# Pairs of tokens in VectorE's transposes, and a way by DRAM for decayed k in twelve units instead of six

## Chip, core and metric

The kernel runs on one core of a Trainium2 chip. Its time is the device time of one execution in microseconds. Five engines work on their own instruction streams and meet through semaphores: PE (TensorE, matmuls and transposes into PSUM), DVE (VectorE), ACT (ScalarE), POOL (GpSimd) and SP (SyncE, which here only issues DMAs).

## What is computed

Two parts follow each other. The first is a gated linear attention over 4 sequences of 768 tokens with 8 heads of width 48:

```
f = sigmoid(f_logit)
state = f[t] * state + k[t] v[t]^T          # one 48 x 48 state per head, token by token
y[t] = q[t] @ state
```

The second is a feed-forward block on the result, laid out as 3072 tokens of width 384, with a hidden width of 1536:

```
g = x @ w_gate
out = (silu(g) * (x @ w_val)) @ w_out
```

Both parts are computed in fp32 and the output is fp32.

## The kernel before

**Chunks and units.** The sequence is cut into 6 chunks of 128 tokens (numbered 0 to 5), and a unit is one batch element of one chunk: unit u = 4 x chunk + batch, 24 in all. `attention(u)` is a generator: each `yield` ends a step, and the caller decides where in the stream of the feed-forward work the next step is put. The recurrence over a chunk becomes matmuls: with cumulative products of the gates, k is scaled by the product of the gates that follow it ("decayed k", tile `kT`) and q by the running product (`qT`), and then scores = kT x qT, masked by `causal`, give `A`; y comes from A x v and from qT x the decayed state.

**From tokens to columns.** The arrays come with tokens on the partitions; the scans and the matmuls want head dimensions on the partitions and tokens along the row. In chunks 0 and 1 PE does those transposes. From chunk 2 on (`SQUARES = 2`) DVE does: it transposes squares of 32 x 32, so the DMA loads f, k and q into `rooms` ("fsquares", "ksquares", "qsquares"), one room each, in such a way that a token t lies at partition and square (t, i) with token number 4t + i. `in_turn` is the view of the output that puts the tokens back into their order: the next element of a transposed row is written four fp32 further on.

**The steps of a unit from chunk 2 on**, each with its line:
- L556 (ACT) sigmoid of the f squares; L565 (DVE) transposes them into `gates`
- L572 (DVE) transposes the k squares into `kT`
- L576 (DVE) the scan from the end of the chunk, into `tails`; L579 a reciprocal
- L584 (DVE) kT = kT x tails
- if the unit is `turned`: L591 (DVE) transposes the squares of kT into `beside`, which is the memory of this unit's qT, and L594 (SP) writes that to the DRAM tile `turn` in four DMAs, in runs of 32 fp32. Units 14 to 19 are turned
- L598 (DVE) the scan from the front, into `gates`
- L601 (DVE) transposes the q squares into `qT`; then `load_after(u)` puts the twelve DMAs for the f, k and q squares of the next unit on SP (L428)
- L604 (DVE) qT = qT x gates, and a small memset on POOL (L605)
- L617 (PE) the scores; in a unit that is not turned, L621 (PE) also transposes kT back to tokens on partitions
- the decayed k with tokens on the partitions, `kt`, comes from PSUM by ACT (L629), or, in a turned unit, from `turn` by one DMA (L627)
- L631 (DVE) the mask; L540 (DVE) the decayed state
- y (L652, L656 on PE for batches 0 to 2, copied by ACT at L660 into `yT` and moved into xT by ten DMAs on SP at L667; L677 on PE for batch 3, which uses `diagonal`, a tile that shares its memory with yT and that POOL clears at L544 and ACT fills at L546)
- L697 (PE) dS = kt x v, the addition to the state; the v of the unit after next is loaded (L432)

`kT` and `kt` have one buffer each, `qT` two, and the rooms one each.

**The feed-forward.** From chunk 1 on, gate and val are computed by fifteen block products in place of eighteen (`mlp_fifteen`, PE at L957): the sums of tokens (`xs`), the sums of weights (`extra`) and the combination of the products (`c`, `aside`, then `h` at L909) are made by DVE (L858, L861, L864) and ACT (L962, L973). The second matrix works by seven products in place of eight (`down_seven`, PE at L1056 and L1119). This is called a block below: block c computes the feed-forward of chunk c, and the attention of chunk c + 1 is put into it.

**What sets the order.** Tables of planned times (`CHAINS`, `SCORES`) give the place of each attention step within the block. All instructions that are traced from there on are then held in that order on PE, DVE, ACT, POOL and SP (`keep_order`). [...]

```
    in_order(mark, (mybir.EngineType.PE, mybir.EngineType.DVE, mybir.EngineType.Activation,
                    mybir.EngineType.Pool, mybir.EngineType.SP))
```

Of the kernel before, what the change touches and what calls it, by code (L numbers as in the profile page):

```python
# [13 lines left out]
ALU = mybir.AluOpType  # L14
# [275 lines left out]
def short_path(ctx, tc, ident, least, judge, q, k, v, f_logit, moe_w_gate, moe_w_val, moe_w_out, out):  # L290
# [9 lines left out]
    nc = tc.nc  # L300
    B, H, S, D = q.shape
    C = 128
    NCH = S // C
    HP = H // 2
# [6 lines left out]
    N1 = C + 1  # L311
# [3 lines left out]
    SQUARES = 2  # L315
# [47 lines left out]
    def pairs(t, off=0):  # L363
        return t[:, off:off + HP * N1].rearrange("p (a t) -> p a t", t=N1)
# [30 lines left out]
    NI = C // Q  # L395
    RUN = NI * D

    rooms = {}
# [9 lines left out]
    def squares(nm):  # L408
        return rooms[nm][:, Q:Q + HP * RUN].rearrange("t (a i e) -> t a i e", a=HP, i=NI)[:, :, :, 0:Q]

    def in_turn(t):

        return t.rearrange("p a (t i) -> p a i t", i=NI)

    def load(u, what="fkqv"):
        b, c = units[u]
        rows = slice(c * C, (c + 1) * C)
        for nm, src in (("f", f_logit), ("k", k), ("q", q), ("v", v)):
            if nm not in what:
                continue  # L420
            if nm == "v":
                dst = v_of(u)
            elif c < SQUARES:
                dst = raw[nm][u % NRAW]
            else:
                for n in range(4):
                    at = Q * (1 - n % 2)
                    nc.sync.dma_start(  # L428
                        out=rooms[nm][Q * n:Q * (n + 1), at:at + HP * RUN].rearrange("t (a e) -> t a e", a=HP),
                        in_=src[b, n // 2::2, rows, :].rearrange("a (t i) d -> t a (i d)", i=NI))  # L430
                continue
            nc.sync.dma_start(out=dst[:, :, 0:D], in_=src[b, :, rows, :].rearrange("h t d -> t h d"))  # L432
# [79 lines left out]
    def rows_of(par):  # L512
        return slice(W * par, W * par + D)
# [3 lines left out]
    def bank(name):  # L517
        return banks[-1].tile([128, 512], FP32, tag="a", name=name)
# [10 lines left out]
    def attention(u):  # L529
        b, c = units[u]  # L530
        fr, kr, qr = (raw[nm][u % NRAW] for nm in "fkq")
        v_ = v_of(u)
        gate, tail = (x[u % NROT if c < SQUARES else 0] for x in (gates, tails))

        diagonal = None

        def decay():
            nonlocal diagonal
            if c:
                nc.vector.tensor_tensor(decayed[:, :, 0:D], states[b], whole.broadcast_to((128, HP, D)), ALU.mult)  # L540
            if c and b == B - 1:

                diagonal = att.tile([128, HP, 2 * D], FP32, tag="x", name="diagonal")
                nc.gpsimd.memset(diagonal, 0.0)  # L544
                for par in range(2):
                    nc.scalar.copy(diagonal[rows_of(par), :, par * D:(par + 1) * D], decayed[rows_of(par), :, 0:D])  # L546

        def transposed(name, src):
            p = bank(name)
            for a in range(HP):  # L550
                nc.tensor.transpose(p[:, a * C:(a + 1) * C],
                                    src[:, 2 * a:2 * a + 2, :].rearrange("t r d -> t (r d)"), ident)
            return p.rearrange("p (a t) -> p a t", t=C)
# [6 lines left out]
        else:  # L560
            p = transposed("fTp", fr)
            nc.scalar.activation(pairs(gate)[:, :, 1:N1], p, AF.Copy if u in ahead else AF.Sigmoid)
        yield
        if c >= SQUARES:
            nc.vector.transpose(in_turn(pairs(gate)[:, :, 1:N1]), squares("f"))  # L565
        yield

        kT = att.tile([128, HP, C], FP32, tag="kT", name="kT")
        qT = att.tile([128, HP, C], FP32, tag="qT", name="qT", bufs=2)
        kp, qp = kT, qT  # L570
        if c >= SQUARES:
            nc.vector.transpose(in_turn(kT), squares("k"))  # L572
        yield

        n = HP * N1
# [5 lines left out]
        if c < SQUARES:  # L581
            kp = transposed("kTp", kr)
            qp = transposed("qTp", qr)
        nc.vector.tensor_tensor(kT, kp, pairs(tail, 2)[:, :, 0:C], ALU.mult)  # L584
        yield
        turned = (SQUARES + 1) * B + 1 < u < (NCH - 1) * B
        if turned:


# [8 lines left out]
        nc.vector.tensor_tensor_scan(gate[:, 0:n], gate[:, 0:n], start, 1.0, op0=ALU.mult, op1=ALU.add)  # L598
        yield
        if c >= SQUARES:  # L600
            nc.vector.transpose(in_turn(qT), squares("q"))  # L601
            load_after(u)
        yield
        nc.vector.tensor_tensor(qT, qp, pairs(gate)[:, :, 1:N1], ALU.mult)  # L604
        nc.gpsimd.memset(pairs(gate)[:, :, 0:1], 0.0)  # L605
        if 0 < c < SQUARES:
            load_after(u)
        if c < SQUARES:
            decay()
# [8 lines left out]
        if c < NCH - 1 and not turned:  # L618
            p = bank("kt")
# [14 lines left out]
        if c >= SQUARES:  # L634
            decay()
# [4 lines left out]
        if c and b < B - 1:  # L640
# [20 lines left out]
            for h in range(H):  # L661
                a, par = h // 2, h % 2
# [31 lines left out]
        if c < NCH - 1:  # L694
            p = bank("dS")
# [13 lines left out]
    def load_after(u):  # L709

        w = u + (1 if units[u][1] >= SQUARES else 2)
        if w < len(units) and (units[w][1] >= SQUARES) == (w == u + 1):
            load(w, "fkqv" if units[w][1] < SQUARES or w == SQUARES * B else "fkq")

    def attention_steps(c):

        runs = [attention(c * B + b) for b in range(B)]
        parts = [3, 6, 3, 3]
        order = sorted((2 * b + s, b, n) for b in range(B) for s, n in enumerate(parts))
        return [lambda b=b, n=n: [next(runs[b]) for _ in range(n)] for _, b, n in order]  # L720
# [445 lines left out]
    mark = traced[-1]  # L1166
    keep_warm(5)
    first = [attention(b) for b in range(B)]
    done = [0] * B

# [82 lines left out]
    for c in range(2, NCH):  # L1253
        for b in range(B):
            run = attention(c * B + b)
            waiting += [((c - 2) * whole + t, lambda run=run: next(run)) for t in times(c)[b]]
# [33 lines left out]
def kernel(  # L1290
# [22 lines left out]
    def judge(bank):  # L1313
# [12 lines left out]
        yield  # L1326

    short_path(tc, ident, least, judge, *args)
    with tc.If(redo[0] > 0):
        general_path(tc, *args)  # L1330
# [32 lines left out]
```

## Time and profile before

| | us |
|---|---|
| median of 3 runs | 610.28 |
| lowest and highest | 609.24, 611.36 |
| the profiled execution, its time | 611.44 |
| the profiled execution, its span | 609.6 |
| PE busy in the span | 595.8 |
| DVE busy | 494.3 |
| ACT busy | 288.5 |
| POOL busy | 7.6 |

The granted clock of PE was 0.996. Times of single instructions come from the profiled execution, counted from the start of its span. Instructions on one engine overlap by about 0.1 us in the records, so the distance between two starts is what an instruction takes of its engine: a 128 x 512 addition on DVE lasts 0.69 us and the next starts 0.60 us after it.

A line of the groups reads: line, engine, operation, output<-input, shapes, count | busy us, mean ns of one | idle time of the engine just before, and what ended it. A line of a timeline reads: start, duration, engine, line, operation, output<-input, count, and in brackets the idle time before it and what ended it. A line of the chain reads: start, us, engine and line. SPq is SP's queue of DMA issues.

### The profile page before, as it was taken

How to read it: one execution, taken by the hardware profiler on the slowest of the kernel's cores; microseconds unless marked ns; L12 is line 12 of the kernel's file. 1: busy time of each engine (PE TensorE's matmuls, PEld its weight loads, DVE VectorE, ACT ScalarE, POOL GpSimd, SP SyncE). 2: the span in 40 equal slices, each digit the busy share in tenths (PEclk: the TensorE clock that was granted, in tenths of full speed). 3: DMA queues.
4: the chain of work that ended last, by engine and by line, in shares of the span. 5: the costliest groups of instructions: out<-in, count | busy, mean ns of one | idle time of the engine just before them, and what ended most of it. 6: DMA issues, size and time to landing. Idle time of an engine off the chain costs nothing.

```text
span 609.6 us, 10796 instructions
## 1 busy us (share of the span) xinstructions
PE 595.8 (98%) x4036; PEld 491.1 (81%) x4036; DVE 494.3 (81%) x833; ACT 288.5 (47%) x554; POOL 7.6 (1%) x52
## 2 busy tenths in 40 slices
PE   7899999999999999999999999999999999999996
PEld 5744545667888799888899988899988899988896
DVE  7999989868999985999996789996878981566731
ACT  3466644313776522476732366742276730366600
POOL 1000000000000000000000000000000000000000
PEclk9999999999999999999999999999999999999999
DMA  9988372005312044323236334145313100100001
GB/s 199 260 194 295 126 247 79 5 15 159 95 39 70 23 108 115 105 53 96 61 89 145 94 97 110 35 112 120 110 44 90 27 6 10 53 1 1 0 1 59
DMA packets 109142, 54.10 MB, mean 89 GB/s; under 512 B 68760, under 2 KB 102168, under 8 KB 109080
## 3 DMA queue, kind: packets, MB, share of 16 engines
q1 hardware_dynamic: 107064, 50.56, 31.3%
q10 hardware_dynamic: 2016, 2.75, 1.2%
q8 instruction: 34, 0.56, 0.4%
q14 instruction: 28, 0.23, 0.1%
HBM read 44.04 MB, written 6.29 MB: 83 GB/s over the span
## 4 chain that ended last, share of the span: by engine, by line
PE 85%; DVE 10%; SPq 1%; issue 1%; DMA 1%; ACT 1%; POOL 0%; DVEq 0%; ACTq 0%; POOLq 0%
PE o L1056 17%; PE A L957 15%; PE B L957 12%; PE gate L755 5%; PE val L755 5%; PE o L957 5%; PE c L957 5%; PE sc L617 4%; PE o L778 3%; PE o L1119 3%; PE y L677 2%; PE y L656 2%; PE dS L697 2%; PE y L652 1%; DVE c L861 1%
## 5 line engine op out<-in xcount | busy, mean ns | idle before, releaser
L1056 PE MATMUL o<-w_out,h 128*128 128x192 f32 x360 | 62.0, 327 | 0.5 <-DVE h L909 0.5
L957 PE MATMUL A<-xs,w_both 128*128 128x256 f32 x240 | 62.1, 381 | 0.0
L1056 PEld LDWEIGHTS o<-w_out,h 128*128 128x128 f32 x360 | 58.7, 190 | 1.7 <-DVE h L909 0.8
L962 ACT COPY c<-A 128x512 f32<-128x512 f32 x40 | 23.3, 583 | 62.6 <-PE A L957 62.6
L962 ACT COPY aside<-A 128x512 f32<-128x512 f32 x60 | 35.1, 584 | 32.6 <-PE A L957 32.6
L858 DVE TENSOR_TENSOR c<-c,aside 128x512 f32<-128x512 f32 x60 | 41.6, 694 | 10.5 <-ACT aside L962 9.0
L957 PEld LDWEIGHTS A<-xs,w_both 128*128 128x128 f32 x240 | 44.9, 190 | 6.5
L909 DVE TENSOR_TENSOR h<-h,c 128x256 f32<-128x256 f32 x100 | 41.1, 419 | 7.3 <-ACT h L973 7.3
L861 DVE TENSOR_TENSOR c<-c,aside 128x512 f32<-128x512 f32 x60 | 41.4, 689 | 2.5 <-ACT aside L962 2.5
L973 ACT ACTIVATE h<-c 128x256 f32<-128x256 f32 x100 | 39.2, 416 | 8.4 <-DVE c L858 5.8
L1056 PE MATMUL o<-ws,h 128*128 128x192 f32 x240 | 41.5, 328 | 0.2 <-DVE A L631 0.2
L957 PE MATMUL B<-xs,w_both 128*128 128x256 f32 x160 | 41.2, 380 | 0.6 <-ACT aside L962 0.6
L957 PE MATMUL c<-xT,w_both 128*128 128x256 f32 x160 | 41.2, 380 | 0.5 <-DVE c L861 0.5
L957 PE MATMUL A<-xs,extra 128*128 128x256 f32 x160 | 41.2, 380 | 0.0
L957 PE MATMUL B<-xT,extra 128*128 128x256 f32 x160 | 41.1, 379 | 0.0
L962 ACT COPY aside<-B 128x512 f32<-128x512 f32 x60 | 35.1, 584 | 11.7 <-PE B L957 7.2
L631 DVE TENSOR_TENSOR A<-sc,causal 128x512 f32<-128x512 f32 x48 | 30.8, 684 | 11.3 <-PE sc L617 11.3
L1056 PEld LDWEIGHTS o<-ws,h 128*128 128x128 f32 x240 | 39.1, 190 | 0.8 <-DVE A L631 0.4
L861 DVE TENSOR_TENSOR c<-o,c 128x512 f32<-128x512 f32 x40 | 27.6, 690 | 10.0 <-ACT h L973 5.8
L957 PEld LDWEIGHTS c<-xT,w_both 128*128 128x128 f32 x160 | 30.3, 190 | 5.0 <-DVE c L861 0.9
L957 PEld LDWEIGHTS B<-xs,w_both 128*128 128x128 f32 x160 | 30.2, 190 | 5.0 <-ACT aside L962 1.0
L957 PEld LDWEIGHTS A<-xs,extra 128*128 128x128 f32 x160 | 30.3, 190 | 4.5 <-ACT c L962 0.4
(138 smaller groups left out, 1140.2 us busy)
## 6 DMA issues: line engine op xcount, KB each, us to landing
fsquares<-in_f_logit_dram SPq DMA_DIRECT2D x64, 96.0 KB, 2.6
ksquares<-in_k_dram SPq DMA_DIRECT2D x64, 96.0 KB, 2.3
qsquares<-in_q_dram SPq DMA_DIRECT2D x64, 96.0 KB, 2.2
v<-in_v_dram SPq DMA_DIRECT2D x24, 192.0 KB, 3.0
w<-in_moe_w_gate_dram SPq DMA_DIRECT2D x6, 768.0 KB, 6.3
w<-in_moe_w_val_dram SPq DMA_DIRECT2D x6, 768.0 KB, 5.1
w<-in_moe_w_out_dram SPq DMA_DIRECT2D x6, 768.0 KB, 5.3
out_dram<-ob ACTq DMA_DIRECT2D x14, 192.0 KB, 2.7
```

The lines of the kernel that those rows point to most:

```text
L617: nc.tensor.matmul(sc[par][:, a * C:(a + 1) * C], lhsT=kT[r, a, :], rhs=qT[r, a, :], start=True, stop=True)
L631: nc.vector.tensor_tensor(A[:, par], sc[par].rearrange("p (a t) -> p a t", t=C), causal.unsqueeze(1).broadcast_to((128, HP, C)), ALU.mult)
L755: nc.tensor.matmul(p, lhsT=w[:, j, i, :], rhs=xT[c][:, i, :], start=(i == 0), stop=(i == KT - 1))
L778: nc.tensor.matmul(p, lhsT=hidden_tile(h, n // 2)[:, n % 2 * 2 + b // 2, b % 2 * C:(b % 2 + 1) * C], rhs=w_out[:, j, :], start=(n == 0), s ...
L858: nc.vector.tensor_tensor(dst, a, b, ALU.add)
L861: nc.vector.tensor_tensor(dst, a, b, ALU.subtract)
L909: lagging.append(lambda: f(*args))
L957: nc.tensor.matmul(p[name][:, n, :], lhsT=weights_of[a][:, n, j, :], rhs=tokens[b], start=fresh and n == 0, stop=True, skip_group_check=True)
L962: nc.scalar.copy(t, p[name])
L973: nc.scalar.activation(dst, src[:, 0, :], AF.Silu)
L1056: nc.tensor.matmul(p[:, n, :], lhsT=lhsTs[j][:, n * C:(n + 1) * C], rhs=rhs[:, j, :], start=first and j == order[0] and n == 0, stop=j == ...
L1119: nc.tensor.matmul(p, lhsT=hidden_tile(h, j)[:, 2, n * C:(n + 1) * C], rhs=b22[:, j, :], start=j == order[0], stop=j == order[-1])
```

## The change

- `split_squares` and `parted` replace the old views in the transposes of k and q: the output of a transpose is laid out as two halves j, each with (head pair, t, i) and i running over 2. Tokens lie in pairs, and the next element of a transposed row is written two fp32 further on. f is transposed as before.
- k is transposed into qT's memory instead of kT's; q into the memory of the k room instead of qT's.
- The products (`multiply`) read the paired layout, take their three operands in the order (head pair, t, j, i), and write kT and qT in the order of the tokens.
- `turned` holds for units 8 to 19.
- `load_after(u)`, with the loads of the next unit's squares, stands after q's product instead of after q's transpose.

```diff
+    def split_squares(nm):
+        return squares(nm).rearrange("t a (j i) e -> t a j i e", j=2)
...
+    def parted(t):
+        return t.rearrange("p (j a t i) -> p a j i t", j=2, a=HP, i=NI // 2)
...
+        def multiply(out, x, by):
+            if c >= SQUARES:
+                for_each = "p a (t j i) -> p a t j i"
+                out, by = (t.rearrange(for_each, j=2, i=NI // 2) for t in (out, by))
+                x = x.rearrange("p (j a t i) -> p a t j i", j=2, a=HP, i=NI // 2)
+            nc.vector.tensor_tensor(out, x, by, ALU.mult)
...
         if c >= SQUARES:
-            nc.vector.transpose(in_turn(kT), squares("k"))
+            kp = qT.rearrange("p a t -> p (a t)")
+            nc.vector.transpose(parted(kp), split_squares("k"))
...
-        nc.vector.tensor_tensor(kT, kp, pairs(tail, 2)[:, :, 0:C], ALU.mult)
-        yield
-        turned = (SQUARES + 1) * B + 1 < u < (NCH - 1) * B
+        multiply(kT, kp, pairs(tail, 2)[:, :, 0:C])
+        yield
+        turned = SQUARES <= c < NCH - 1
...
         if c >= SQUARES:
-            nc.vector.transpose(in_turn(qT), squares("q"))
-            load_after(u)
-        yield
-        nc.vector.tensor_tensor(qT, qp, pairs(gate)[:, :, 1:N1], ALU.mult)
+            qp = rooms["k"][:, 0:HP * C]
+            nc.vector.transpose(parted(qp), split_squares("q"))
+        yield
+        multiply(qT, qp, pairs(gate)[:, :, 1:N1])
         nc.gpsimd.memset(pairs(gate)[:, :, 0:1], 0.0)
-        if 0 < c < SQUARES:
+        if c:
             load_after(u)
```

On the engines' streams this takes 24 transposes off PE and 6 copies off ACT, adds 6 transposes on DVE, and adds 30 DMAs on SP (24 `turn<-qT`, 6 `kt<-turn`). On SP each unit's turn DMAs stand before the loads of the next unit's squares, and its kt DMA after them (after the xT and v DMAs too, where those follow). In unit 12 the load of v for unit 13 now stands before the squares of unit 13.

## The prediction

> **What bounds the kernel now.** I read the page first, busy shares and the chain that ended last; then the groups of instructions by form, the chain in order of time, and timelines of single engines around the units (unit = 4 x chunk + batch; chunks 2 to 4 are units 8 to 19). Busy shares, then the chain's shares by engine:
>
> ```profile
> PE 595.8 (98%) x4036; PEld 491.1 (81%) x4036; DVE 494.3 (81%) x833; ACT 288.5 (47%) x554; POOL 7.6 (1%) x52
> PE 85%; DVE 10%; SPq 1%; issue 1%; DMA 1%; ACT 1%; POOL 0%; DVEq 0%; ACTq 0%; POOLq 0%
> ```
>
> PE is full almost throughout; its order is written out, so it has nothing to put in place of an instruction that waits. Whatever takes PE work away gains, and whatever comes late for PE costs its whole delay. The groups:
>
> ```profile
> L572 DVE STREAM_TRANSPOSE kT<-ksquares 128x512 f32<-128x512 f32 x16 | 17.8, 1113 | 0.0
> L601 DVE STREAM_TRANSPOSE qT<-qsquares 128x512 f32<-128x512 f32 x16 | 18.0, 1125 | 6.4 <-DMA turn<-qT 6.4
> L591 DVE STREAM_TRANSPOSE qT<-kT 128x512 f32<-128x512 f32 x6 | 4.2, 702 | 0.0
> L629 ACT COPY kt<-kt 128x512 f32<-128x512 f32 x14 | 8.2, 585 | 16.7 <-PE kt L621 16.7
> ```
>
> L591 writes 32-element rows and takes 702 ns; L572 and L601 write every fourth element and take 0.41 us more. L601 also waited 6.4 us for `turn` to be written: that is the price of the way by DRAM. DVE's timeline shows these waits, SP's the queue ahead of them (unit 14, then 16):
>
> ```profile
> 275.14 2.63 SPq L594 DMA_DIRECT2D turn<-qT  x4
> 279.52 1.15 DVE L601 STREAM_TRANSPOSE qT<-qsquares 128x512 f32<-128x512 f32 x1 [0.58 <-DMA turn<-qT]
> ...
> 321.75 2.61 SPq L594 DMA_DIRECT2D turn<-qT  x4
> 328.31 1.13 DVE L601 STREAM_TRANSPOSE qT<-qsquares 128x512 f32<-128x512 f32 x1 [2.69 <-DMA turn<-qT]
> ```
>
> From the first issue of `turn` until DVE may write qT again, call it T: 4.4 us for unit 14, 6.6 for 16 (SP full before it), 6.2 for 17, at most 4.7 for 18. Last, the end of chunk 2 in the chain of waits, where SP itself is the path:
>
> ```profile
> 223.99 1.09 PE sc L617 x16
> 228.05 1.43 SPq L667
> 233.34 1.79 DMA xT<-yT
> 236.17 2.12 PE y L677 x56
> ```
>
> SP issues without a pause from 213.1 to 235: ten xT pieces of unit 9, v, twelve squares, ten xT pieces of unit 10 (226.85, 7.08 us). When these have landed POOL clears `diagonal` (235.31), ACT fills it, and PE's y of unit 11 starts at 236.17, having waited 0.3.
>
> [...] L473, reading every second word, takes 554 ns for 384 columns and 956 for 768, 1.05 ns a column. Writes at step two are not in the trace. [...] `turn` goes in 128 B runs and lands 3.1 us after an issue, q squares (768 B) after 2.2.
>
> **The change, part by part.**
>
> *32 transposes of k and q.* Bounds 0.70 (L591) and 1.11 us; I take 0.70. Start to start that is 0.95 to 0.60: 0.35 less each, 11 us of DVE. It hardly reaches PE, whose stalls lie in 178 to 210 (30.46 of 32 us busy) and about nowhere later. The 32 products read pairs: 0.69 as before[...].
>
> *kt of units 8 to 13 leaves PE and ACT.* In the chain, unit 8 with PE's transposes, then unit 18 without:
>
> ```profile
> 158.30 1.09 PE sc L617 x16
> 159.98 1.73 PE A L957 x8
> ...
> 385.67 1.09 PE sc L617 x16
> 386.76 1.06 PE A L957 x4
> 387.82 0.86 PE B L957 x4
> ```
>
> With them 0.59 lies between scores and next product; without, that product takes 0.20 more. Saved: 0.39 a unit, 2.35 for six. ACT's six copies (3.5 us) I count as nothing: ACT is 47% busy and PE there waits for none of them. POOL keeps its instructions.
>
> *What comes in:* six L591 transposes (0.60 a start on DVE), 24 turn and 6 kt DMAs on SP (2.63 + 0.67 us a unit), and three new orders. q's product, no longer q's transpose, waits for `turn`; behind it stand DVE's additions, the mask and, on PE, the scores. k and q loads of the next unit wait for q's product, because its room holds q; behind them on SP stand xT, v, kt and the next turn. k's transpose writes qT, free once y of two units earlier is done: everywhere so, counted as nothing.
>
> *Unit 8.* k's product starts 0.35 earlier (151.46), two additions, then L591 from 153.4 to 154.1. SP is idle, so T = 5.0 (between 4.4 and 6.2): q's product at 159.15, not 157.39. Its scores started 0.84 after it (158.23); now 160.0. **+1.75** (+1.15 to +3.35).
>
> *Units 8 and 9 without kt:* **-0.78**. In 178 to 209 DVE sets the pace; unit 10 there has two transposes less 0.35 and one more of 0.60, -0.1 net; DVE starts that stretch with its mask +1.36, so PE's second 0.39 is mostly lost: **+0.3**. The shift at 209 is 1.26; below, times are those of before, with the shift left out.
>
> *Unit 11.* SP first finishes unit 9's xT and v (220.9), then kt of unit 10, and reaches turn at 221.7. SP was full, as before unit 16: T = 6.6, q's product at 228.3, scores at 229.1 in place of 223.92. It doesn't end there. Unit 12's k loads wait for that product: 229.05, k and q 3.75, xT of unit 10 from 232.8 instead of 226.85. `diagonal`, and with it y of unit 11, comes 5.95 later: **+5.9**. PE's own delay and kt of units 10 and 11 (0.78) disappear under it. Of the 5.9, 3.3 are the five DMAs put in front of xT. With T = 4.4 and xT issued at 0.59 a piece it is +2.5. kt of unit 11 is issued at about 240.5, in time for 244.
>
> *Unit 12:* turn from 241, q's product near 246.6. State, outputs and token sums are behind it; those have 1.7 us of slack to PE: 0. *Unit 13:* k's product at 254.5, turn at 256.45, T = 5.0, scores at 262.3 instead of 261.7: +0.6, which swallows unit 12's 0.39; unit 13's comes off: **+0.2**. *Unit 16:* k loads wait for 312.2 instead of issuing at 306.1, so xT and turn go 2.3 later; scores 331.45 instead of 331.22: **+0.3**. Units 14 to 19 lose waits of 6.4 us on DVE that PE did not feel: 0.
>
> Sum: 1.75 - 0.78 + 0.3 + 5.9 + 0.2 + 0.3 = **+7.65 us**. The profiled execution took 611.44 (span 609.6), hence 619.1; the median of the runs is 1.16 lower, so I forecast 617.9.
>
> **The rivals.**
> - *Main case, slower by 4.5 to 9 us* (614.8 to 619.3): 0.55.
> - *Shallow:* T = 4.4 everywhere, SP as quick as elsewhere: 1.15 - 0.78 + 0.3 + 2.5 - 0.8 = +2.4, 612.7. For it: units 14 and 18. Against: unit 16, with the same queue ahead of it. From +1.8 to +4.5: 0.20.
> - *Deep:* T = 6.6 everywhere (+1.6 at unit 8, +1.6 at unit 13), and transposes that stay at 1.11 us (the change not doing what it says: +0.35 at units 8 and 13 and +0.7 at unit 10, where DVE paces): +12, 622. 0.12.
> - *Faster:* DVE gets to q's product after `turn` has landed and SP has room. Then PE's 2.35 comes in, with up to 1.5 of DVE stalls: 606.4 to 607.9. It decides at T under 3.3 us in unit 8 (154.15 to 157.4), and a turn for unit 11 issued by 218. Against it: three earlier issues take 2.0 us and the shortest landing seen is 2.1. 0.08.
> - *No change,* gains and waits cancelling within 0.3% (1.8 us, about what a measurement of this kernel can tell from no change): 0.05.
>
> Range 612.0 to 621.8: from the shallow end to nearly the deep one; left out are the faster and unchanged cases and the last of the deep one, 0.19.
>
> **What would show it.** Right: transposes of k and q near 0.70; no kt matmuls after unit 7; q's products of units 8 and 11 waiting for `turn`, 2 and 5 us or more; scores of unit 11 and then its y waiting on PE, DMA xT and SPq in the chain between them; PE busy less by 2 to 6 us. Wrong: y of unit 11 without a wait of some us, or a PE gap anywhere after chunk 3 that is larger than 2 us.

## The result, and the profile after

| | us |
|---|---|
| changed kernel, median of 7 runs | 624.88 (624.16 to 629.87) |
| kernel before beside it, median of 7 runs | 610.37 (609.24 to 611.36) |
| ratio, with its 95% interval | 1.0255 (1.0235 to 1.0274) |
| the profiled execution of the changed kernel, its span | 629.87, 628.1 |

The changed kernel is slower by 2.55%, about 15.6 us at 610.4 (14.5 by the medians); the forecast was 7.65. The profiled execution is the longest of the seven. Its granted clock was 0.982, that of the others 0.987 to 0.992, so its sums are some 5 us larger than the median's.

Busy shares, the granted clock in 40 slices and the chain by engine, from the page of the changed kernel:

```profile
PE 599.5 (95%) x4012; PEld 493.1 (79%) x4012; DVE 486.5 (77%) x839; ACT 285.2 (45%) x548; POOL 7.6 (1%) x52
PEclk8999999999899988999999999999999999999999
PE 69%; DVE 14%; SPq 7%; DMA 5%; issue 2%; ACT 1%; DVEq 0%; POOL 0%; ACTq 0%; POOLq 0%
```

PE has 24 instructions less and is busy 3.7 us more. The 8s of the clock row at 157 to 173 us and at 220 to 251 hold the reason: from 161.8 for 3.4 us and from 230.1 for 10.2 us the records show half the clock, which they did not show there before (granted clock 0.53 from 161.7 to 165.3 and 0.51 from 230.0 to 240.4; before 1.00 in both places). PE's share of the chain fell from 85% to 69%; SP's queue and DMA, 2% together before, have 12%. The groups by form, then the waits (engine, line, waited for, us in total, times, longest):

```profile
L590 DVE STREAM_TRANSPOSE qT<-ksquares 128x512 f32<-128x512 f32 x16 | 11.2, 703 | 0.8 <-DMA ksquares<-in_k_dram 0.8
L620 DVE STREAM_TRANSPOSE ksquares<-qsquares 128x512 f32<-128x512 f32 x16 | 11.2, 697 | 0.0
L552 DVE TENSOR_TENSOR qT<-ksquares,gates 128x512 f32<-128x512 f32 x16 | 11.0, 686 | 22.9 <-DMA turn<-qT 22.8
```

```profile
ACT fsquares L573 <- DMA fsquares<-in_f_logit_dram: 30.5, 5, 8.8
PE sc L635 <- DVE qT L552: 6.7, 6, 2.0
PE dS L715 <- DMA kt<-turn: 5.3, 2, 3.8
PE o L1074 <- ACT ob L1100: 3.8, 2, 2.0
```

The transposes of k and q cost what L591 cost before, and the products are no slower. The losses are in the last three lines: scores that wait for q's product (2.5 us before), dS that waits for `kt`, and a matrix product of the feed-forward that waits for ACT to empty a bank. Neither of the last two waits was there before. ACT waits for the f squares 30.5 us in place of 16.1.

Comparing the start of each PE instruction with its start before gives the places: +2.0 at the scores of unit 8, +4.0 at dS of unit 10, +1.6 at the scores of unit 11, +1.6 at its dS, +0.8 net at unit 13, +2.3 and +1.8 in the down products of units 15 and 19, about +4.1 for work at half clock behind units 8 and 11, +0.9 for another piece of half clock near 13 us (granted clock 0.53 from 11.6 to 15.2), where nothing was changed; -0.3 to -0.5 for each `kt` that left PE. Together PE ends 18.1 us late in the profiled execution. The timelines of SP and of PE at the end of chunk 2:

```profile
216.88 7.35 SPq L685 DMA_DIRECT2D xT<-yT  x10
...
224.91 0.61 SPq L645 DMA_DIRECT2D kt<-turn  x1
225.62 2.94 SPq L612 DMA_DIRECT2D turn<-qT  x4
...
236.66 6.93 SPq L685 DMA_DIRECT2D xT<-yT  x10
...
244.27 0.60 SPq L645 DMA_DIRECT2D kt<-turn  x1
```

```profile
230.68 1.10 PE L715 MATMUL dS<-v,kt 128*64 128x48 f32 x16 [3.76 <-DMA kt<-turn]
233.05 2.08 PE L635 MATMUL sc<-qT,kT 48*128 48x128 f32 x16 [1.27 <-DVE qT L552]
...
248.01 0.86 PE L695 MATMUL y<-qT,diagonal 128*32 128x128 f32 x24
...
251.26 0.67 PE L715 MATMUL dS<-v,kt 128*64 128x48 f32 x16 [1.50 <-DMA kt<-turn]
```

`kt` of unit 10 stands behind ten xT pieces and v, is issued at 224.91 and is used at 230.68; `kt` of unit 11 goes at 244.27 and is used at 251.26. The y at 248.01 doesn't wait: PE is that late already. In this stretch the chain that ended last does not run through PE's waits at unit 10. It runs on SP from the xT pieces of unit 9 (issued from 216.88) to `turn` of unit 11, then over q's product (232.21), the k and q squares of unit 12, xT of unit 10 and v to `kt` of unit 11, and reaches PE at dS (251.26). Its two longest pieces:

```profile
227.72 4.37 DMA turn<-qT
...
244.27 6.94 DMA kt<-turn
```

Units 15 and 19 lose in another way. SP, ACT and PE in unit 15:

```profile
325.99 1.74 SPq L437 DMA_DIRECT2D ksquares<-in_k_dram  x4
327.78 1.85 SPq L437 DMA_DIRECT2D qsquares<-in_q_dram  x4
329.73 7.62 SPq L685 DMA_DIRECT2D xT<-yT  x10
```

```profile
339.22 0.71 ACT L563 COPY diagonal<-decayed 48x192 f32<-48x192 f32 x2 [11.70 <-POOL diagonal L561]
339.95 0.48 ACT L1100 COPY ob<-o 128x384 f32<-128x384 f32 x1
```

```profile
340.49 4.17 PE L1074 MATMUL o<-ws,hs 128*128 128x192 f32 x24 [1.99 <-ACT ob L1100]
```

Squares of unit 16 wait on SP for q's product; the xT pieces stand behind them; `diagonal` waits for these; ACT's copy of `ob` stands behind the fill of `diagonal`; and PE's next product needs the bank that this copy empties.

### The profile page after: what moved, and what is told of

Read it like the earlier page. It is cut to its first block, busy times and chain, and to the rows that moved or that the text cites. A ratio compares the mean times of both kernels' runs of the same rounds, so it can differ in the third digit from the quotient of the medians.

```text
span 628.1 us, 10792 instructions
## 1 busy us (share of the span) xinstructions
PE 599.5 (95%) x4012; PEld 493.1 (79%) x4012; DVE 486.5 (77%) x839; ACT 285.2 (45%) x548; POOL 7.6 (1%) x52
## 4 chain that ended last, share of the span: by engine, by line
PE 69%; DVE 14%; SPq 7%; DMA 5%; issue 2%; ACT 1%; DVEq 0%; POOL 0%; ACTq 0%; POOLq 0%
PE A L975 13%; PE o L1074 12%; PE B L975 11%; PE gate L773 5%; PE val L773 5%; PE c L975 4%; PE o L975 4%; PE sc L635 3%; SPq L685 3%; PE o L796 3%; SPq L437 3%; PE o L1137 2%; PE y L695 2%; DVE c L879 2%; DMA turn<-qT 2%
## 5 line engine op out<-in xcount | busy, mean ns | idle before, releaser
L1074 PE MATMUL o<-w_out,h 128*128 128x192 f32 x360 | 62.0, 328 | 0.5 <-DVE h L927 0.5
L1074 PEld LDWEIGHTS o<-w_out,h 128*128 128x128 f32 x360 | 58.7, 190 | 1.7 <-DVE h L927 0.8
L1074 PE MATMUL o<-ws,h 128*128 128x192 f32 x240 | 43.8, 340 | 0.7 <-DVE A L649 0.7
L1074 PEld LDWEIGHTS o<-ws,h 128*128 128x128 f32 x240 | 41.3, 199 | 1.5 <-DVE A L649 1.0
L635 PE MATMUL sc<-qT,kT 48*128 48x128 f32 x384 | 29.6, 293 | 7.8 <-DVE qT L552 6.7
L635 PEld LDWEIGHTS sc<-qT,kT 48*128 48x128 f32 x384 | 24.7, 194 | 13.3 <-issue 6.8
L876 DVE TENSOR_TENSOR c<-c,o 128x384 f32<-128x384 f32 x15 | 8.3, 551 | 34.3 <-PE o L1074 34.3
```

What stands on the lines that cost most here:

```text
L635: nc.tensor.matmul(sc[par][:, a * C:(a + 1) * C], lhsT=kT[r, a, :], rhs=qT[r, a, :], start=True, stop=True)
L876: nc.vector.tensor_tensor(dst, a, b, ALU.add)
L1074: nc.tensor.matmul(p[:, n, :], lhsT=lhsTs[j][:, n * C:(n + 1) * C], rhs=rhs[:, j, :], start=first and j == order[0] and n == 0, stop=j == ...
```

## The experiments

Theory A: the loss is in the DRAM way of units 8 to 13, about 10 us, and about 4 us come from the order of loads at units 15 and 19. Rival B: the loads' wait for q's product is the main loss everywhere. Rival C: the paired forms are slow. The last column is the ratio less one, times 610.4. "New loads" means squares of the next unit behind q's product.

| run | DRAM way in units | transposes, loads | median us | ratio (95%) | to before, us |
|---|---|---|---|---|---|
| changed | 8-19 | paired, new loads | 624.88 | 1.0255 (1.0235-1.0274) | +15.6 |
| e1 | 14-19 | paired, new loads | 612.36 | 1.0032 (1.0022-1.0042) | +2.0 |
| e2 | 8-19 | as before | 629.23 | 1.0303 (1.0263-1.0343) | +18.5 |
| e3 | 8-19 | 15, 19, 23 as before for q | 623.87 | 1.0197 (1.0161-1.0232) | +12.0 |
| e4 | 8, 9, 12-19 | as changed | 618.11 | 1.0124 (1.0094-1.0153) | +7.6 |
| e5 | 8-19 | as changed, idle matmuls | 627.60 | 1.0280 (1.0250-1.0310) | +17.1 |
| e6 | 8-19 | as changed, kt on ACT's queue | 631.56 | 1.0335 (1.0313-1.0357) | +20.4 |
| e7 | 9, 12, 14-19 | as e3 | 609.06 | 0.9977 (0.9967-0.9988) | -1.4 |
| e8 | 14-19 | as e3 | 609.33 | 0.9983 (0.9973-0.9992) | -1.0 |
| e9 | 8, 9, 11-19 | as changed | 621.62 | 1.0183 (1.0158-1.0209) | +11.2 |
| e10 | 8-10, 12-19 | as changed | 622.54 | 1.0207 (1.0178-1.0236) | +12.6 |
| e11 | 9-12, 14-19 | as changed | 623.54 | 1.0212 (1.0189-1.0234) | +12.9 |
| e12 | 8, 13, 14-19 | as e3 | 613.21 | 1.0058 (1.0037-1.0079) | +3.5 |

**e1, pairs without the new units.**

```diff
-        turned = SQUARES <= c < NCH - 1
+        turned = (SQUARES + 1) * B + 1 < u < (NCH - 1) * B
```

> The changed kernel with its DRAM way for decayed k kept to units 14 to 19, as before the change; the paired transposes and the later loads of the next unit's squares stay. Theory A (most of the 14.5 us is lost in units 8 to 13: products of q, kt of units 10 and 11 and their followers late behind turn in SP's queue, with half clocks after two of the waits, about 10 us; the rest, about 4 us, in units 15 and 19, where the next unit's squares hold up xT on SP, hence diagonal and ACT's ob copy): 4 to 5 us above the kernel before, 614 to 615; waits of PE L1074 for ACT L1100 near 325 and 419 remain, no half clock near 162 and 230. Rival B (the loads' wait for q's product, everywhere, is the main loss): 10 us or more above before, 620 or later. Rival C (paired forms are slow in themselves): about 14 above before.

Measured +2.0: the pairs and new loads carry little, and 13.6 of the 15.6 us go with the units moved. C falls, and B falls for the loads by themselves. With `turn` in front of it q's product comes later, and the loads behind it with it: that share of the 13.6 was not separated, since in e2 the loads wait with q's transpose instead. DVE was busy 483.1 us, 11.2 less than before, as 32 x 0.35 asks. A was right on where and too high on how much, in part since the pairs give about a microsecond back (e8). The two waits of L1074 are there, 3.0 us together:

```profile
PE o L1074 <- ACT ob L1100: 3.0, 2, 1.7
```

**e2, the new units without the pairs**: the diff of e1 reversed, made in the kernel before.

> The kernel before with the DRAM way for decayed k in units 8 to 19, and nothing else of the change: transposes at a step of four tokens, loads of the next unit's squares right after q's transpose. Here it is q's transpose that waits for turn. Theory A: 10 to 12 us above the kernel before, 620 to 622, lost at units 8, 10, 11 and 13, and no wait of L1074 for ACT at units 15 and 19. Rival B: at most 3 us above before, since the order of the loads is the old one. Rival C: at most 1 above.

Measured +18.5, more than the whole change. Theory A had the sign and missed by 7 us. With q's transpose into qT, both transpose and product stand behind `turn`; PE's timeline at unit 8, where the changed kernel waited 2.0:

```profile
162.36 2.08 PE L617 MATMUL sc<-qT,kT 48*128 48x128 f32 x16 [4.06 <-DVE qT L604]
```

In e2 1.85 us lie between the start of q's transpose, when the wait ends (159.78), and q's product (161.63): the transpose and two more instructions of DVE. In the changed kernel they are done before the wait. So putting q into the room of k, together with the faster form, is worth some 2 us at unit 8. That part of the change does its work.

**e3, old order of q and loads in units 15, 19 and 23.**

```diff
-        if c >= SQUARES:
+        plain = c > SQUARES and b == B - 1
+        if plain:
+            nc.vector.transpose(in_turn(qT), squares("q"))
+            load_after(u)
+        elif c >= SQUARES:
...
```

> The changed kernel, but units 15, 19 and 23 transpose q as before into qT at a step of four tokens, and the next unit's squares are loaded right after that transpose. Theory A: the two waits of PE L1074 for ACT L1100 (2.3 and 1.8 us) go, 4 us less than the changed kernel, about 621. Rival (ACT's copy is late for another reason, for example the xT pieces themselves): no change within 1 us. Rival B: much more than 4 less.

In e3's trace both waits for `ob` are gone. The ratio falls by 3.5 us, the median by only 1.0, and the intervals just miss each other. The same edit on top of e1 (that is e8) was measured better: 612.36 to 609.33, 3.0 us. For these two units the chain load, xT, `diagonal`, `ob` is shown.

**e4, units 10 and 11 back on PE.**

```diff
-        turned = SQUARES <= c < NCH - 1
+        turned = SQUARES <= c < NCH - 1 and u not in (10, 11)
```

> The changed kernel with kt of units 10 and 11 made by PE and ACT again; everything else stays. Theory A: the waits of dS for kt in units 10 and 11 (4.0 and 1.6 us), that of the scores of unit 11 (1.6) and the half clock near 230 to 240 (about 2.9) go, and 0.4 a unit of PE work comes back: 7 to 9 us less than the changed kernel, 616 to 618. Rival B: within 1 us of the changed kernel, the loads still wait for q's product. Rival D (the half clock comes at its own times, not after waits of PE): 5 to 6 less, and a half clock in this stretch remains.

6.8 us by the median, 8.0 by the ratio: theory A. No half clock was left in this stretch (24 matmuls of L1074 took 4.17 us from 227.31, where the changed kernel took 6.35 from 235.87), and the profiled clock was 0.997, so rival D falls. That showed what half a clock had covered in the changed kernel. SP ahead of unit 9 of e4, then DVE, ACT, PE in it:

```profile
152.79 3.74 SPq L612 DMA_DIRECT2D turn<-qT  x4
156.63 2.00 SPq L437 DMA_DIRECT2D fsquares<-in_f_logit_dram  x4
```

```profile
163.28 1.13 DVE L582 STREAM_TRANSPOSE gates<-fsquares 128x512 f32<-128x512 f32 x1 [1.67 <-DMA qsquares<-in_q_dram]
```

```profile
161.26 1.28 ACT L573 ACT_TABLE_LOAD   x1 [3.71 <-DMA fsquares<-in_f_logit_dram]
```

```profile
172.75 1.13 PE L975 MATMUL c<-xT,w_both 128*128 128x256 f32 x4 [1.67 <-ACT c L980]
```

Unit 9's f squares stand on SP behind the four issues of `turn`. They do not wait for unit 8's product of q, which starts at 158.18, after they are issued; the k squares (158.90) do. ACT's copies for the feed-forward stand behind the sigmoid of f, DVE's additions behind its transpose, and PE waits once more, 14 us after the scores. DVE comes to this point late by the wait of q's product (2.19) and by the 1.67 for f. (The releaser named in the DVE line is a DMA of q; the sigmoid of f had ended at 163.2, just before.)

**e5, idle matmuls on PE ahead of three waits**, against the half clock.

```diff
+        warm(sc[0], {8: 8, 11: 6}.get(u, 0))
...
+            warm(p, 16 if u == 10 else 0)
```

> The changed kernel with idle matmuls (bf16, results never read) on PE ahead of the three long waits: 8 before the scores of unit 8, 6 before those of unit 11, 16 before dS of unit 10. The waits themselves stay. Clock theory (PE standing still for 2 us or more brings the half clock, in some executions; it costs 4 to 5 of the 14.5 us): no half clock near 162 and 230, granted clock 0.995 or more in all runs, 620 to 621.5. Rival (the half clock comes from elsewhere, or is what the busy stretch brings): clock near 0.988 as in the changed kernel, 625 or more.

The 2 us of the clock theory come from the wait of 2.01 at unit 8 of the changed kernel, with half clock behind it. The clock was kept, 0.992 to 0.997 in all four runs, and the time was not: 627.6. PE in e5, at full clock until 250:

```profile
244.48 1.12 PE L701 MATMUL y<-qT,diagonal 128*32 128x128 f32 x21 [0.83 <-ACT diagonal L568]
...
248.75 0.67 PE L722 MATMUL dS<-v,kt 128*64 128x48 f32 x16 [2.16 <-DMA kt<-turn]
```

A PE that is not slowed arrives earlier and waits for SP's chain instead: y waits for `diagonal`, and dS longer for `kt`. So the theory that half a clock costs 4 to 5 of the 14.5 us falls; in this stretch it mostly fills time that the transfers take anyway. e5 is 1.5 us above the changed kernel by the ratio, but the two intervals overlap, so no difference is shown; whether the idle matmuls hold PE up themselves was not tried.

**e6, `kt` read on ACT's queue.**

```diff
-                nc.sync.dma_start(out=kt, in_=turn.rearrange("t i a r e -> i t (a r e)"))
+                nc.scalar.dma_start(out=kt, in_=turn.rearrange("t i a r e -> i t (a r e)"))
```

> The changed kernel with the DMA that reads kt from turn issued on ACT's queue, so that kt of unit 10 need not stand behind the ten xT pieces and v on SP. If kt's place in SP's queue is the one binding thing at chunk 2's end: the wait of dS of unit 10 (4.0 us) and the half clock after it go, 5 to 7 us less, 618 to 620. If the turn of unit 11 binds at nearly the same time (my theory): kt of unit 10 lands near 221, the scores of unit 11 then wait some 4 us in its stead, and the time falls by 1 to 3 us, 622 to 624.

Both expectations missed: 4.9 us more than the changed kernel by the ratio. At the place in question it went as the theory has it:

```profile
227.73 0.62 PE L715 MATMUL dS<-v,kt 128*64 128x48 f32 x16
...
247.62 1.12 PE L695 MATMUL y<-qT,diagonal 128*32 128x128 f32 x21 [2.05 <-ACT diagonal L563]
```

dS of unit 10 no longer waits; the scores of unit 11 wait 2.21 (at 230.55), and y of unit 11, which now waits 2.05 for `diagonal`, starts at 247.62 in place of 248.01. So 0.4 of the 4.0 us is left. The further loss stands later: L1074 in units 15 and 19 waited 2.56 and 3.10 us for `ob`, with half clock behind that of unit 15 (15 matmuls in 4.29 us, where the changed kernel has 24 in 4.17). Why these waits grew was not tried.

**e9, e10: unit 10 or unit 11 alone back on PE** (the edit of e4 with one number).

> The changed kernel, but unit 10 makes kt on PE and ACT again; unit 11 keeps the DRAM way. Theory A' (the half clock is not the cause; turn and loads of unit 11, with xT of unit 10 behind them, are): the wait of dS for kt of unit 10 goes, but the scores of unit 11 wait some 4 us instead of 1.6 and y of unit 11 stays where it is: 0 to 2 us less than the changed kernel, 623 to 625. Rival (kt of unit 10 is the loss): 4 to 5 less, about 620.

> The changed kernel, but unit 11 makes kt on PE and ACT again; unit 10 keeps the DRAM way. Theory A': no turn stands between kt of unit 10 and the squares of unit 12 on SP, so kt of unit 10 lands sooner (a wait of dS of 2 to 3.5 us), the waits of the scores (1.6) and of dS in unit 11 (1.6) go and y of unit 11 comes earlier: 4 to 6 us less, 619 to 621. Rival (kt of unit 10 is the loss): 2 less at most, 623 or more.

4.4 and 2.9 us less by the ratio, 8.0 for both: they add up, nearly. The expectation that unit 11 alone was the loss falls, and so does its reverse. In e10 no turn followed `kt` of unit 10 on SP; it was issued at 224.18 and dS still waited until 231.03:

```profile
231.03 1.09 PE L715 MATMUL dS<-v,kt 128*64 128x48 f32 x16 [4.72 <-DMA kt<-turn]
```

So the writes of `turn` behind it are not what makes `kt` slow. Its own bytes go in large pieces: the DMA view of the changed kernel from 224 to 232 us has 3651 packets, of which 128 are of 2 KB or more, one for each partition of `kt`:

```profile
DMA packets 3651, 0.94 MB, mean 118 GB/s; under 512 B 3205, under 2 KB 3523, under 8 KB 3651
```

Whether `kt` is late by itself or by the small packets of the xT pieces ahead of it in the queue was not separated. In e9 the scores of unit 11 waited 2.55.

**e11, units 8 and 13 back on PE; e12, these two alone.**

> The changed kernel, but units 8 and 13 make kt on PE and ACT again; units 9 to 12 keep the DRAM way. In the trace of the changed kernel unit 8 costs 2.0 and unit 13 1.1 us, and each gains 0.3 to 0.4 of PE work. Theory A' (what unit 8 loses is swallowed where SP's chain holds y of unit 11, unless SP itself is late by it): 1 to 3 less, 622 to 624. Rival (unit 8's delay is carried whole, with DVE's additions behind it late too): 3 to 4.5 less, 620.5 to 622.

> The run with paired transposes, q plain in units 15, 19 and 23, and the DRAM way in units 14 to 19 (609.3 us), with units 8 and 13 given the DRAM way besides: what the two cost when nothing after them covers it. Theory A' (the product's wait also holds back the squares of units 9 and 14, so that DVE and ACT are late with work for PE afterwards): unit 8 +3.7, unit 13 +1.8 by the trace of the run without units 10 and 11, 5 to 6 more, 614 to 615.5. Rival (the waits of the scores alone, less the PE work saved: 2.0 + 1.1 - 0.8): 2 to 3 more, 611.5 to 612.5.

e11 is 2.6 us under the changed kernel by the ratio (1.3 by the medians), as its theory A' had it. e12 is 4.6 above e8 by the ratio, 3.9 by the medians: between its two expectations, and not decided. The mechanism that its theory A' names, f squares held by q's product, is not what its trace shows: SP issues those of unit 9 at 156.64, behind `turn` (152.83, 3.71 us), and the product starts at 158.19. That units 8 and 13 cost 4.6 us alone and 2.6 in the changed kernel says that the later losses cover some of theirs. PE in e12 lost 2.05 at unit 8 and 1.0 at unit 13, and won 0.3 to 0.5 with each `kt`; the lower granted clock, 0.997 in its profiled execution and 0.999 in e8's, makes some 1.2 us more, an estimate (0.002 x 610).

**e7, e8: what is left when the waits are taken out.**

> Paired transposes of k and q, units 15, 19 and 23 with q transposed as before and loads after that transpose, and the DRAM way in units 9, 12 and 14 to 19 alone (units 8, 10, 11 and 13 make kt on PE and ACT). Theory A: none of the long waits is left, 0.8 us of PE work (units 9 and 12) is off, DVE is faster: 1 to 2 us under the kernel before, 608.5 to 609.5. Rival (moving even one unit costs a wait that the trace of the changed kernel hides under others): at or above 611.

> As the run before it, but with the DRAM way in units 14 to 19 alone, as before the change: the paired transposes by themselves, without the later loads where these hurt. Theory A: 0 to 1 us under the kernel before, 609.4 to 610.4, and 0.8 above the run before it. Rival C (pairs cost something in themselves): above 611.5.

Both beat the kernel before, by 1.4 us (0.7 to 2.0) and 1.0 (0.5 to 1.6). Units 9 and 12, which add the DRAM way in e7, lie within the uncertainty: 0.3 us. e7's waits of the scores:

```profile
PE sc L642 <- DVE qT L552: 2.8, 3, 1.2
```

No wait of dS and none for `ob` is left.

## Why the prediction was right or wrong

The direction and the main place were right, the size was half of what came.

**Right.** The price of a transpose (0.70; measured 0.703 and 0.697) and of a product (0.69; 0.673 and 0.686). That a transpose writing at a step of two would take what L591 takes for rows (702 ns) was the author's estimate; no trace of before has such a write. T in unit 8 was put at 5.0 and was 5.4 (154.99 to 160.39); in unit 11 at 6.6, and was 6.6 (225.62 to 232.21). The scores of unit 8 lost 2.0 for a forecast of 1.75. In e5, where the clock hides nothing there, y of unit 11 starts at 244.48; the working had 236.17 + 1.26 + 5.95 = 243.4. The chain from `turn` over squares and xT to `diagonal` was priced to 1.1 us, though in the changed kernel it is `kt` and not `diagonal` that it ends in. Each `kt` off PE gave 0.3 to 0.5, forecast 0.39. Unit 12 is 0 and unit 16 a few tenths, as forecast; for unit 12 this is slack more than price, since T was 7.3 there (245.53 to 252.85) and some 5.6 in the working. Two slips of the working change little: its sum as written is 7.67, and the upper end at unit 8, +3.35, belongs to T = 6.6 and not to 6.2.

Its own sign of being wrong came true: y of unit 11 did not wait. `diagonal` was filled at 246.4 and y began at 248.01; PE had lost its time at dS of unit 10 and at the scores, and lost more at dS of unit 11.

**Wrong, the landing of `kt`.** The step that failed first is "kt of unit 11 is issued at about 240.5, in time for 244"; for unit 10 there was no step at all. The DMA's issue was counted (0.67 us), its landing was not: the page gave none, the six reads of `kt` before had 9.5 us or more until dS and never showed one, and 3.5 us were thought enough. From issue until dS could start it was 5.8 us (unit 10) and 7.0 (unit 11) in the changed kernel, 6.9 in e10, 5.7 in e9. PE lost 4.0 and 1.6 us by it in the profiled execution, but the 4.0 at unit 10 are covered by the chain that ends at unit 11, as e6 bears out. With its shift of 1.26 the prediction has dS of unit 11 at 245.4; it came at 251.26. Of these 5.8 us 2.5 were there when `kt` was issued (244.27 for 241.8), as SP began the xT pieces of unit 9 3.8 us later than before (216.88 for 213.11) and not 1.26, and 3.3 are the landing.

**Wrong, what stands behind `turn` and q's product.** The prediction followed the loads for units 11 and 16 alone. At unit 8 it counted the scores and "+0.3" for the stretch of 178 to 209; at full clock PE lost 1.67 more at 172.75 (e4), by q's product and by f squares that stood behind `turn` on SP. At unit 13 "+0.2" was +0.8, and not by T, which was 4.2 (269.09 to 273.29) for a forecast of 5.0: the scores waited 0.73 for an addition of DVE that stands behind q's product. And "Units 14 to 19 ... 0" was wrong: they lose their waits on DVE, but in units 15 and 19 ACT's copy of `ob`, behind `diagonal`, costs 3.0 us by e8 against e1. The copies of ACT on either side of `diagonal` were in no step.

**Wrong, PE's busy time.** It was to fall by 2 to 6 us and rose by 3.7. No term stood for the clock. Nor does a run show the fall at full clock: e8, with every kt matmul of the kernel before, was busy 593.1 us, e7 with 8 fewer 593.0, e4 with 16 fewer 594.6; the record of before, 595.8, has a piece of half clock at 28.0 us (granted clock 0.57 from 28 to 32).

By the runs: DRAM way of units 8 to 13, forecast 1.75 - 0.78 + 0.3 + 5.9 + 0.2 = +7.4, measured 15.6 - 2.0 = +13.6; the rest, forecast +0.3, measured +2.0, as 3.0 lost by the loads and 1.0 won by e8, where the prediction had the faster transposes hardly reach PE. Of the 13.6, 8.0 go with units 10 and 11 (e4), forecast 5.9, and the 5.6 left are those of units 8, 9, 12 and 13, forecast 1.5. How the miss divides between the two steps depends on which units are taken out first, since the losses cover each other (e11 and e12). The rival "deep" had 622 by T = 6.6 everywhere and slow transposes; neither was so, and it came nearer for the wrong reason.

## What to carry to other kernels

A transfer that replaces engine work has a landing as well as an issue, and the use at the far end must be checked for each unit against both; here the second half, DRAM to SBUF, took about as long as the first (5.8 and 7.0 us at units 10 and 11, T 6.6 at unit 11). When a wait or new issues are put ahead of loads, follow the written order of every engine from what they load, to the copy that frees another stage's bank: in unit 15 ACT stood 11.70 us before `diagonal`, and PE 1.99 for the `ob` behind it. And when a stall is removed or a slow stretch sped up, look for the next late arrival before counting the gain: e5 and e6 removed what they meant to and gained nothing.

## What the runs showed of the hardware that was not expected

- One DMA of 256 KB from DRAM to SBUF, in 128 pieces of 2 KB behind a full SP queue, took 5.7 to 7.0 us from issue to use where PE waited for it (the changed kernel, e9, e10).
- Around PE waits of 2.01 us (unit 8) and 3.76 us (unit 10) the records of the changed kernel show half the clock for 3.4 and 10.2 us, one and three pieces of 3.41. The wait at unit 8 had it in the changed kernel (2.01) and not in e3 (1.99) and e4 (2.00), where the scores after it took 1.16 us instead of 1.47; with idle matmuls put in (e5) it was gone at these places (scores of units 8 and 11 in 1.16, dS of unit 10 in 0.67). What brings it was not shown: the record of before has a piece at 28.0 us, where PE's longest wait nearby was 0.79.
- Transposes that write every second fp32 ran at the rate of those that write in a row: 697 to 703 ns against 706 (L609), and 1113 to 1125 for every fourth (before).
